# Low weights of two products 32 bytes further on, and their matmul first: a retention and mixture-of-experts kernel

## The chip, the cores and the metric

The kernel runs on one core of a Trainium2 chip. Its time is the device time of one launch in microseconds (us), and a version stands for the median of several runs. PE is TensorE, PEld its weight loads, DVE is VectorE, ACT ScalarE, POOL GpSimd and SP the engine that issues the DMAs.

## The reference, cut to what matters

```python
attn_out = _attn_ref(q, k, v, lam)            # (2, 8, 768, 64): retention with a decaying state
x = attn_out.transpose(0, 2, 1, 3).reshape(1536, 512)
P = balanced(exp(x @ w_gate))                 # 8 rounds of row and column scaling, (1536, 8)
for e in range(8):                            # the part that this change touches
    h = np.maximum(x @ w1[e], 0.0)            # (1536, 512) @ (512, 1024)
    out += P[:, e:e + 1] * (h @ w2[e])        # (1536, 1024) @ (1024, 512)
h = out @ w_in                                # a last dense layer, 512 -> 2048 -> 512
return (h - np.tanh(h)) @ w_out
```

All of it is float32. The kernel keeps float32 accuracy by splitting each operand into a high part (rounded by ScalarE) and a low part (the rest, by VectorE), and adding three matmuls: high by high, high by low, low by high.

## The kernel before, in words

After the attention come 96 steps (`NS`), one for each half of an expert's hidden layer and each of three blocks of 512 tokens. A step computes `x @ w1` by seven products of a Strassen scheme (1, 2, 5, 6, 7, 4, 3, in this order). `product` runs each as six matmuls of 256 columns: for each of the two halves `k` of the inner dimension high by high (L579), high weights by low tokens (L581), low weights by high tokens (L582). The stationary operand is always the weight piece (`w1h`, `w1l`), the moving one the tokens (`xph`, `xpl` for products 1, 2 and 3, `xsh`, `xsl` for the others). Products 1, 6, 7 and 4 are written to `ha`, products 2, 5 and 3 to `hb`.

Twice in a step, ahead of product 7 and ahead of product 4, stand the matmuls of `second` for the step before: 12 of 512 columns each (L477, L478, L480), with the hidden values (`hhia`, `hloa`, `hhib`, `hlob`) stationary, `w2h` and `w2l` moving, and the sums in `yp`. So one step is, on PE: products 1, 2, 5, 6 (24 matmuls), 12 matmuls of `second`, product 7 (6), 12 of `second`, products 4 and 3 (12): 42 short matmuls and 24 long ones, in the order in which the code calls them. Ahead of each matmul stands the load of its weights.

`w1_split` fills the weight tiles some steps ahead: ScalarE copies to `w1h`, VectorE subtracts into `w1l` (L132 and L133 in the helper `split`). `WI` says at which column of the tiles a product's 256 weights begin. In bytes from the start of a partition and modulo 256, the built program has the token tiles at 160, the weight tiles `w1h` and `w1l` at 224, and `w2h`, `w2l` and the hidden tiles at 32. A half of 128 weights is 512 bytes, so all pieces of products 1, 2, 5, 6, 7 and 3 begin at 224, and those of product 4, whose `WI` is 8 columns (32 bytes) more than a multiple of 256, at 0.

```python
WI = {1: 0, 2: 256, 3: 1280, 4: 1536 + 8, 5: 512, 6: 768, 7: 1024}
```

The last dense layer (L686 to L688) has its own weights and is not touched.

Of the kernel before, what the change touches and what calls it, by code (L numbers as in the profile page):

```python
# [8 lines left out]
F32 = mybir.dt.float32  # L9
F32R = mybir.dt.float32r  # L10
# [3 lines left out]
ACTF = mybir.ActivationFunctionType  # L14
ALU = mybir.AluOpType
# [18 lines left out]
PAD = 16  # L34
PADC = 48
W1C = 7 * 256 + 64


TSW = 0.625
# [3 lines left out]

WI = {1: 0, 2: 256, 3: 1280, 4: 1536 + 8, 5: 512, 6: 768, 7: 1024}
XI = {1: ("p", 0), 2: ("p", 1), 3: ("p", 2), 4: ("s", 3), 5: ("s", 0), 6: ("s", 1), 7: ("s", 2)}


# [1 line left out]
def kernel(  # L51
# [9 lines left out]
    nc = tc.nc  # L61
# [5 lines left out]
    wps = [ctx.enter_context(tc.tile_pool(name="wpa", bufs=1))]  # L67
# [28 lines left out]
    wraw, wsum, w1h, w1l, w2h, w2l = {}, {}, {}, {}, {}, {}  # L96
# [8 lines left out]
    def w_sum(q, eng):  # L105
        a11, a12, a22, a21 = (wraw[q][:, 256 * i:256 * i + 256] for i in range(4))
        wsum[q] = stg.tile([128, 1024], F32, tag="sum", name=f"wsum{q}")
        s1, s2, s3, s4 = (wsum[q][:, 256 * i:256 * i + 256] for i in range(4))
        eng.tensor_tensor(out=s1, in0=a21, in1=a22, op=ALU.add)
        eng.tensor_tensor(out=s3, in0=a11, in1=a21, op=ALU.subtract)  # L110
        eng.tensor_tensor(out=s2, in0=s1, in1=a11, op=ALU.subtract)
        eng.tensor_tensor(out=s4, in0=a12, in1=s2, op=ALU.subtract)


    def pad(pool, name, n=PAD):
        if name not in padded:
            padded[name] = pool.tile([128, n], F32, tag=name, name=name)
# [3 lines left out]
    def w1_alloc(q):  # L121
        pad(wps[q % 3], f"pada{q % 3}", (PAD, PAD + 32, PAD + 8)[q % 3])
        w1h[q] = wps[q % 3].tile([128, W1C], F32R, tag="w1h", name=f"w1h{q}")
        w1l[q] = wps[q % 3].tile([128, W1C], F32R, tag="w1l", name=f"w1l{q}")

    def w2_alloc(q):
        pad(wps[q % 3], f"padb{q % 3}")
# [3 lines left out]
    def split(hi, lo, src, eng=nc.vector):  # L131
        nc.scalar.activation(out=hi, in_=src, func=ACTF.Copy)  # L132
        eng.tensor_tensor(out=lo, in0=src, in1=hi.bitcast(F32), op=ALU.subtract)  # L133

    def w1_split(q, part):
        if part == 0:
            w1_alloc(q)
        if q < 2 * NU:
            for o, src in (((WI[1], wraw[q][:, 0:512]), (WI[4], wraw[q][:, 512:768])), ((WI[5], wsum[q]),))[part]:
                n = slice(o, o + src.shape[1])  # L140
                split(w1h[q][:, n], w1l[q][:, n], src)
        else:
            n, m = (slice(c, c + 512) for c in (512 * part, 512 * part + PADC))
            split(w1h[q][:, m], w1l[q][:, m], wraw[q][:, n], nc.gpsimd)
# [36 lines left out]
    for i in range(12):  # L181
# [9 lines left out]
        out=g[:, 129:257], data0=lamt.to_broadcast([H, 128]), data1=one8, initial=1.0,  # L191
# [7 lines left out]
        out=dtab,  # L199
        in_=bass.AP(tensor=gbase.tensor, offset=gbase.offset, ap=[[1, 128], [384, H], [1, 128]]),  # L200
# [3 lines left out]
    for hh in range(2):  # L204
        src = gscr[:, 129:257].rearrange("(n two) m -> two n m", two=2)[hh]
        nc.sync.dma_start(
            out=lq[64 * hh:64 * hh + 64],
            in_=src.rearrange("(o n) m -> o n m", o=1).to_broadcast([64, NP, 128]),
# [9 lines left out]
    scps, at, s1, xr, qd = {}, {}, {}, {}, {}  # L218
# [114 lines left out]
    def gate2(b):  # L333
# [9 lines left out]
    }  # L343
    wt = {
        1: lambda: w_load(0), 3: lambda: w_sum(0, nc.vector), 5: lambda: w1_split(0, 0), 6: lambda: w1_split(0, 1),
        7: lambda: (w2_split(0, 0), w2_split(0, 1), w_load(1)), 10: lambda: w_sum(1, nc.gpsimd),
    }
    def ahead(c):
# [182 lines left out]
    for u in range(NU + NQ):  # L531
        s0 = 6 * (u - 1)
        q0, q1 = 2 * u, 2 * u + 1
        strassen = u < NU
        if u > 0:
            fill[s0 + 2].append(lambda q=q0: w_load(q))
            if strassen:
                fillc[s0 + 2].append(lambda q=q0: w_sum(q, nc.gpsimd))
            s0 += u == 1
            for i in range(2):  # L540
                (fill, fillb)[i][s0 + 3].append(lambda q=q0, i=i: w1_split(q, i))
            for i in range(2):
                (fill, fillb)[i][s0 + 4].append(lambda q=q0, i=i: w2_split(q, i))
            fillb[s0 + 4].append(lambda q=q1: w_load(q))
            if strassen:
                fillc[s0 + 4].append(lambda q=q1: w_sum(q, nc.gpsimd))
            for i in range(2):
                (fill, fillb)[i][s0 + 5].append(lambda q=q1, i=i: w1_split(q, i))
        for i in range(2):
            (fill, fillb)[i][max(s0 + 6, 1)].append(lambda q=q1, i=i: w2_split(q, i))  # L550
# [21 lines left out]
    def product(ps, s, i, start):  # L572
        u, b, p = s // 6, s // 2 % 3, s % 2
        q = 2 * u + p
        kind, xi = XI[i]
        xh, xl = (x1[b][kind, j][:, xi].rearrange("p (k m) -> p k m", k=2) for j in range(2))
        for k in range(2):
            ws = slice(WI[i] + 128 * k, WI[i] + 128 * k + 128)
            nc.tensor.matmul(out=ps, lhsT=w1h[q][:, ws], rhs=xh[:, k], start=start and k == 0, stop=False,  # L579
                             skip_group_check=True)  # L580
            nc.tensor.matmul(out=ps, lhsT=w1h[q][:, ws], rhs=xl[:, k], start=False, stop=False, skip_group_check=True)  # L581
            nc.tensor.matmul(out=ps, lhsT=w1l[q][:, ws], rhs=xh[:, k], start=False, stop=k == 1, skip_group_check=True)  # L582

    pend = None
    for s in range(NS):
# [7 lines left out]
        u, b, p = s // 6, s // 2 % 3, s % 2  # L593
        q = 2 * u + p
        pa, pb = bank(f"ha{s}"), bank(f"hb{s}")
        s12 = sn_.tile([128, 512], F32, tag="s12", name=f"s12_{s}")
        s5 = sn_.tile([128, 256], F32, tag="s5", name=f"s5_{s}")
        lo, hi = slice(0, 256), slice(256, 512)
        product(pa[:, lo], s, 1, True)
        nc.scalar.activation(out=s12[:, lo], in_=pa[:, lo], func=ACTF.Copy)  # L600
        if pend:
            hb = relu_hi(pend[0], f"b{s - 1}")
            lb = relu_lo(pend[0], hb, f"b{s - 1}")
            parts.append(pend[1] + (hb, lb, False, (s - 1) % 2 == 1))
        product(pb[:, lo], s, 2, True)
        product(pb[:, hi], s, 5, True)
        nc.scalar.activation(out=s5, in_=pb[:, hi], func=ACTF.Copy)
        product(pa[:, lo], s, 6, False)
# [35 lines left out]
    def sub(v):  # L644
        u, b, f = NU + v // 12, v // 4 % 3, v % 4
        return u, b, 2 * u + f // 2, f % 2, f
# [32 lines left out]
    for v in range(NV + 2):  # L679
        if v < NV:  # L680
            u, b, q, i, f = sub(v)
            ph = bank(f"g{v}")
            for k in range(KT):
                blk = {(0, 0): 0, (0, 1): 1, (1, 1): 2, (1, 0): 3}[i, k // 2]
                ws = slice(PADC + 256 * blk + 128 * (k % 2), PADC + 256 * blk + 128 * (k % 2) + 128)
# [60 lines left out]
```

## Time and profile before

| what | value |
|---|---|
| median of 3 runs | 1327.33 us (1326.79 to 1328.92) |
| the profiled execution's own time | 1328.56 us |
| its span, first to last instruction | 1326.8 us |
| matmuls on PE | 8383 |
| busy VectorE, ScalarE, GpSimd | 913.0, 527.6 and 274.6 us |
| mean granted TensorE clock | 0.996 |

Matmuls overlap in the records: a record is longer than the distance from its start to the next one's, and its end is modelled. What a matmul costs is read from the starts.

### The profile page before, as it was taken

The numbers are of one execution on the slowest core, as the hardware profiler recorded it, in microseconds if no ns is written. First come the engines' busy times: TensorE is split into PE (matmuls) and PEld (weight loads), VectorE is DVE, ScalarE is ACT, GpSimd is POOL, SyncE is SP. The second block draws the span as 40 slices with busy tenths as digits, with TensorE's granted clock in tenths as the row PEclk, the third lists the DMA queues.
The fourth block names the chain that finished last, engine by engine and source line by source line (L and its number), as shares of the span: only waits on it lengthen the run. The fifth ranks groups of instructions, "written<-read, shape, count | busy, mean of one in ns | idle before, by whom it ended". The sixth has DMA issues, their size and how long they took to land.

```text
span 1326.8 us, 20925 instructions
## 1 busy us (share of the span) xinstructions
PE 1314.7 (99%) x8383; PEld 1163.6 (88%) x8383; DVE 913.0 (69%) x1698; ACT 527.6 (40%) x1029; POOL 274.6 (21%) x323
## 2 busy tenths in 40 slices
PE   8999999999999999999999999999999999999998
PEld 6789999999999999999999999999999888888887
DVE  4976666757667575767666675757654487788887
ACT  1443333223323232323322332323232578776764
POOL 4611011212123131212212221322210102020200
PEclk8999999999999999999999999999999999999999
DMA  9501111212312121212222132221210110010101
GB/s 299 171 33 33 33 61 34 71 56 68 97 46 93 57 68 57 80 56 68 72 64 68 57 99 69 68 68 57 68 36 33 32 33 32 32 32 32 32 33 64
DMA packets 37138, 85.00 MB, mean 64 GB/s; under 512 B 4136, under 2 KB 13872, under 8 KB 37040
## 3 DMA queue, kind: packets, MB, share of 16 engines
q1 hardware_dynamic: 37040, 83.67, 19.8%
q8 instruction: 65, 1.06, 0.3%
q14 instruction: 33, 0.27, 0.1%
HBM read 72.11 MB, written 11.55 MB: 63 GB/s over the span
## 4 chain that ended last, share of the span: by engine, by line
PE 96%; DVE 2%; DMA 1%; issue 0%; ACT 0%; POOL 0%; DVEq 0%; POOLq 0%
PE yp L480 16%; PE yp L477 16%; PE yp L478 16%; PE ha L579 7%; PE ha L582 7%; PE ha L581 7%; PE hb L581 5%; PE hb L579 5%; PE hb L582 5%; PE g L688 3%; PE g L686 3%; PE g L687 3%; PE sc L236 1%; DMA dtab<-gscr 0%; DVE at L242 0%
## 5 line engine op out<-in xcount | busy, mean ns | idle before, releaser
L508 ACT ACTIVATE hhia<-ha 128x512 fp32r<-128x512 f32 x96 | 57.5, 599 | 469.9 <-PE ha L582 464.3
L579 PE MATMUL ha<-xsh,w1h 128*128 128x256 f32 x576 | 162.5, 282 | 1.8 <-ACT s L600 1.3
L582 PE MATMUL ha<-xsh,w1l 128*128 128x256 f32 x576 | 161.3, 280 | 0.0
L581 PE MATMUL ha<-xsl,w1h 128*128 128x256 f32 x576 | 160.9, 279 | 0.0
L456 POOL TENSOR_TENSOR c<-c,d 128x256 f32<-128x256 f32 x64 | 47.8, 747 | 544.3 <-DVE d L455 544.3
L478 PE MATMUL yp<-w2l,hhia 128*128 128x512 f32 x384 | 149.4, 389 | 0.0
L480 PE MATMUL yp<-w2h,hloa 128*128 128x512 f32 x384 | 149.3, 389 | 0.0
L477 PE MATMUL yp<-w2h,hhia 128*128 128x512 f32 x384 | 149.3, 389 | 0.0
L480 PE MATMUL yp<-w2h,hlob 128*128 128x512 f32 x380 | 148.6, 391 | 0.0
L478 PE MATMUL yp<-w2l,hhib 128*128 128x512 f32 x380 | 147.9, 389 | 0.0
L477 PE MATMUL yp<-w2h,hhib 128*128 128x512 f32 x380 | 147.8, 389 | 0.0
L615 DVE TENSOR_TENSOR ha<-ha,s 128x256 f32<-128x256 f32 x96 | 41.4, 432 | 141.8 <-PE ha L582 141.8
L625 DVE TENSOR_TENSOR hb<-hb,s 128x512 f32<-128x512 f32 x96 | 67.0, 698 | 91.3 <-PE hb L582 91.3
L495 DVE SCALAR_TENSOR_TENSOR yacc<-yp,prob,yacc 128x512 f32<-128x512 f32 x168 | 118.8, 747 | 9.0 <-PE yp L480 9.0
L579 PEld LDWEIGHTS ha<-xsh,w1h 128*128 128x128 f32 x576 | 108.4, 188 | 9.6 <-ACT s L600 1.5
L581 PEld LDWEIGHTS ha<-xsl,w1h 128*128 128x128 f32 x576 | 108.5, 188 | 7.4
L582 PEld LDWEIGHTS ha<-xsh,w1l 128*128 128x128 f32 x576 | 109.1, 189 | 0.0
L579 PE MATMUL hb<-xph,w1h 128*128 128x256 f32 x384 | 106.6, 278 | 0.0
L581 PE MATMUL hb<-xpl,w1h 128*128 128x256 f32 x384 | 106.3, 277 | 0.0
L582 PE MATMUL hb<-xph,w1l 128*128 128x256 f32 x384 | 106.1, 276 | 0.0
L480 PEld LDWEIGHTS yp<-w2h,hloa 128*128 128x128 f32 x384 | 72.1, 188 | 15.0
L480 PEld LDWEIGHTS yp<-w2h,hlob 128*128 128x128 f32 x380 | 71.3, 188 | 14.9
(159 smaller groups left out, 3332.6 us busy)
## 6 DMA issues: line engine op xcount, KB each, us to landing
wraw<-in_w SPq DMA_DIRECT2D x64, 512.0 KB, 4.8
d<-in_wio SPq DMA_DIRECT2D x64, 256.0 KB, 2.9
qkv<-in_qkv SPq DMA_DIRECT2D x23, 512.0 KB, 6.9
wscr<-c SPq DMA_DIRECT2D x64, 128.0 KB, 1.8
wraw<-wscr SPq DMA_DIRECT2D x16, 512.0 KB, 4.3
out<-yacc SPq DMA_DIRECT2D x12, 256.0 KB, 2.1
qkv<-in_qkv SPq DMA_DIRECT2D x2, 256.0 KB, 3.3
dtab<-gscr SPq DMA_DIRECT2D x1, 512.0 KB, 6.5
```

The costliest lines, as they stand in the source:

```text
L456: nc.gpsimd.tensor_tensor(out=c1.bitcast(F32), in0=c1.bitcast(F32), in1=lo.bitcast(F32), op=ALU.mult)
L477: nc.tensor.matmul(out=yp, lhsT=a[:, ts], rhs=w2h[q][:, i], start=first, stop=False)
L478: nc.tensor.matmul(out=yp, lhsT=a[:, ts], rhs=w2l[q][:, i], start=False, stop=False)
L480: nc.tensor.matmul(out=yp, lhsT=c[:, ts], rhs=w2h[q][:, i], start=False, stop=last)
L495: nc.vector.scalar_tensor_tensor(out=y, in0=yp[t], scalar=prob[:, b * TPB + t, u // 2:u // 2 + 1], in1=y, op0=ALU.mult, op1=ALU.add)
L508: nc.scalar.activation(out=a, in_=ps, func=ACTF.Relu)
L579: nc.tensor.matmul(out=ps, lhsT=w1h[q][:, ws], rhs=xh[:, k], start=start and k == 0, stop=False, skip_group_check=True)
L581: nc.tensor.matmul(out=ps, lhsT=w1h[q][:, ws], rhs=xl[:, k], start=False, stop=False, skip_group_check=True)
L582: nc.tensor.matmul(out=ps, lhsT=w1l[q][:, ws], rhs=xh[:, k], start=False, stop=k == 1, skip_group_check=True)
L615: nc.vector.tensor_tensor(out=pa[:, hi], in0=pa[:, lo], in1=s5, op=ALU.add)
L625: nc.vector.tensor_tensor(out=pb, in0=pb, in1=s12, op=ALU.add)
L686: nc.tensor.matmul(out=ph, lhsT=w1h[q][:, ws], rhs=x2[b][0][:, k], start=k == 0, stop=False)
```

## The change

It does four things. `LI` gives the low weights a place of their own: for products 7 and 4 the low weights of the first half (`k` = 0) begin at column 1288 and 1608, 32 bytes past the usual place modulo 256, and the second half at the usual one (`w1l` gets 64 columns more). Product 4's high weights, and the second half of its low ones, go back to the usual place. In `product` the matmul with the low weights comes first of the three. To let `w1_split` write the new places, products 3 and 7 trade columns (and `w_sum` two of its slices), and the subtraction for the four summed pieces becomes two instructions.

```diff
--- before.py
+++ after.py
@@ -34,6 +34,7 @@
 PAD = 16
 PADC = 48
 W1C = 7 * 256 + 64
+W1L = 7 * 256 + 128
 
 
 TSW = 0.625
@@ -43,7 +44,11 @@
 
 
 
-WI = {1: 0, 2: 256, 3: 1280, 4: 1536 + 8, 5: 512, 6: 768, 7: 1024}
+
+WI = {1: 0, 2: 256, 3: 1024, 4: 1536, 5: 512, 6: 768, 7: 1280}
+LI = {i: (o, o + 128) for i, o in WI.items()}
+LI[7] = (1288, 1472)
+LI[4] = (1608, 1792)
 XI = {1: ("p", 0), 2: ("p", 1), 3: ("p", 2), 4: ("s", 3), 5: ("s", 0), 6: ("s", 1), 7: ("s", 2)}
 
 
@@ -105,7 +110,7 @@
     def w_sum(q, eng):
         a11, a12, a22, a21 = (wraw[q][:, 256 * i:256 * i + 256] for i in range(4))
         wsum[q] = stg.tile([128, 1024], F32, tag="sum", name=f"wsum{q}")
-        s1, s2, s3, s4 = (wsum[q][:, 256 * i:256 * i + 256] for i in range(4))
+        s1, s2, s4, s3 = (wsum[q][:, 256 * i:256 * i + 256] for i in range(4))
         eng.tensor_tensor(out=s1, in0=a21, in1=a22, op=ALU.add)
         eng.tensor_tensor(out=s3, in0=a11, in1=a21, op=ALU.subtract)
         eng.tensor_tensor(out=s2, in0=s1, in1=a11, op=ALU.subtract)
@@ -121,7 +126,7 @@
     def w1_alloc(q):
         pad(wps[q % 3], f"pada{q % 3}", (PAD, PAD + 32, PAD + 8)[q % 3])
         w1h[q] = wps[q % 3].tile([128, W1C], F32R, tag="w1h", name=f"w1h{q}")
-        w1l[q] = wps[q % 3].tile([128, W1C], F32R, tag="w1l", name=f"w1l{q}")
+        w1l[q] = wps[q % 3].tile([128, W1L], F32R, tag="w1l", name=f"w1l{q}")
 
     def w2_alloc(q):
         pad(wps[q % 3], f"padb{q % 3}")
@@ -136,9 +141,20 @@
         if part == 0:
             w1_alloc(q)
         if q < 2 * NU:
-            for o, src in (((WI[1], wraw[q][:, 0:512]), (WI[4], wraw[q][:, 512:768])), ((WI[5], wsum[q]),))[part]:
-                n = slice(o, o + src.shape[1])
-                split(w1h[q][:, n], w1l[q][:, n], src)
+            def low(i):
+                o, step = LI[i][0], LI[i][1] - LI[i][0]
+                return w1l[q][:, o + 128 - step:o + 128 + step].rearrange("p (k m) -> p k m", k=2)[:, :, step - 128:]
+
+            if part == 0:
+                split(w1h[q][:, 0:512], w1l[q][:, 0:512], wraw[q][:, 0:512])
+                split(w1h[q][:, 1536:1792].rearrange("p (k m) -> p k m", k=2), low(4),
+                      wraw[q][:, 512:768].rearrange("p (k m) -> p k m", k=2))
+            else:
+                nc.scalar.activation(out=w1h[q][:, 512:1536], in_=wsum[q], func=ACTF.Copy)
+                hi = w1h[q].bitcast(F32)
+                nc.vector.tensor_tensor(out=w1l[q][:, 512:1280], in0=wsum[q][:, 0:768], in1=hi[:, 512:1280], op=ALU.subtract)
+                h, w = (a.rearrange("p (k m) -> p k m", k=2) for a in (hi[:, 1280:1536], wsum[q][:, 768:1024]))
+                nc.vector.tensor_tensor(out=low(7), in0=w, in1=h, op=ALU.subtract)
         else:
             n, m = (slice(c, c + 512) for c in (512 * part, 512 * part + PADC))
             split(w1h[q][:, m], w1l[q][:, m], wraw[q][:, n], nc.gpsimd)
@@ -576,10 +592,11 @@
         xh, xl = (x1[b][kind, j][:, xi].rearrange("p (k m) -> p k m", k=2) for j in range(2))
         for k in range(2):
             ws = slice(WI[i] + 128 * k, WI[i] + 128 * k + 128)
-            nc.tensor.matmul(out=ps, lhsT=w1h[q][:, ws], rhs=xh[:, k], start=start and k == 0, stop=False,
+            wl = slice(LI[i][k], LI[i][k] + 128)
+            nc.tensor.matmul(out=ps, lhsT=w1l[q][:, wl], rhs=xh[:, k], start=start and k == 0, stop=False,
                              skip_group_check=True)
-            nc.tensor.matmul(out=ps, lhsT=w1h[q][:, ws], rhs=xl[:, k], start=False, stop=False, skip_group_check=True)
-            nc.tensor.matmul(out=ps, lhsT=w1l[q][:, ws], rhs=xh[:, k], start=False, stop=k == 1, skip_group_check=True)
+            nc.tensor.matmul(out=ps, lhsT=w1h[q][:, ws], rhs=xh[:, k], start=False, stop=False, skip_group_check=True)
+            nc.tensor.matmul(out=ps, lhsT=w1h[q][:, ws], rhs=xl[:, k], start=False, stop=k == 1, skip_group_check=True)
 
     pend = None
     for s in range(NS):
```

On PE, at the end of the first `second` in a step and in product 7 behind it. Before:

```order
L480 MATMUL yp_1_3_6972<-w2h_6664,hloa_7034 128x512
L579 MATMUL ha_7039<-xsh_96,w1h_6335 128x256
L581 MATMUL ha_7039<-xsl_97,w1h_6335 128x256
L582 MATMUL ha_7039<-xsh_96,w1l_6336 128x256
L579 MATMUL ha_7039<-xsh_96,w1h_6335 128x256
L581 MATMUL ha_7039<-xsl_97,w1h_6335 128x256
L582 MATMUL ha_7039<-xsh_96,w1l_6336 128x256
```

And with the change, at the same place:

```order
L496 MATMUL yp_1_3_6992<-w2h_6684,hloa_7055 128x512
L596 MATMUL ha_7060<-xsh_96,w1l_6354 128x256
L598 MATMUL ha_7060<-xsh_96,w1h_6353 128x256
L599 MATMUL ha_7060<-xsl_97,w1h_6353 128x256
L596 MATMUL ha_7060<-xsh_96,w1l_6354 128x256
L598 MATMUL ha_7060<-xsh_96,w1h_6353 128x256
L599 MATMUL ha_7060<-xsl_97,w1h_6353 128x256
```

The matmul with the low weights (`w1l`) moved from third to first in each half, in this and all other products; the number of matmuls is the same. The first L596 is the only one of these six whose weights stand at 0 modulo 256; the others stand at 224. In product 4 it is the same, where before all six stood at 0.

On VectorE, the four-piece subtraction for the same weights (`wsum` are the summed pieces). Before:

```order
L133 TENSOR_TENSOR w1l_1325<-wraw_1109,w1h_1324 128x512
L133 TENSOR_TENSOR w1l_1325<-wraw_1109,w1h_1324 128x256
L133 TENSOR_TENSOR w1l_1325<-wsum_1158,w1h_1324 128x1024
```

And with the change:

```order
L138 TENSOR_TENSOR w1l_1327<-wraw_1111,w1h_1326 128x512
L138 TENSOR_TENSOR w1l_1327<-wraw_1111,w1h_1326 128x2x128
L155 TENSOR_TENSOR w1l_1327<-wsum_1160,w1h_1326 128x768
L157 TENSOR_TENSOR w1l_1327<-wsum_1160,w1h_1326 128x2x128
```

The instruction of 1024 columns became one of 768 and one of 256 in two strips; this happens 32 times. On ScalarE, GpSimd and SP no instruction is added, removed or moved.

## Rows read from the trace of the kernel before

**Rows 1.** The page, part 1 (busy time of engines) and part 4 (chain by engine).

```profile
PE 1314.7 (99%) x8383; PEld 1163.6 (88%) x8383; DVE 913.0 (69%) x1698; ACT 527.6 (40%) x1029; POOL 274.6 (21%) x323
...
PE 96%; DVE 2%; DMA 1%; issue 0%; ACT 0%; POOL 0%; DVEq 0%; POOLq 0%
```

**Rows 2.** Timeline of PE, one step: start, duration, line, matmul.

```profile
559.00 0.39 PE L477 MATMUL yp<-w2h,hhia 128*128 128x512 f32 x1
...
561.72 0.28 PE L579 MATMUL ha<-xsh,w1h 128*128 128x256 f32 x1
...
562.43 0.39 PE L477 MATMUL yp<-w2h,hhib 128*128 128x512 f32 x1
...
564.92 0.40 PE L480 MATMUL yp<-w2h,hlob 128*128 128x512 f32 x1
565.16 0.28 PE L579 MATMUL ha<-xsh,w1h 128*128 128x256 f32 x1
...
565.86 0.28 PE L579 MATMUL hb<-xph,w1h 128*128 128x256 f32 x1
...
566.21 0.28 PE L579 MATMUL hb<-xph,w1h 128*128 128x256 f32 x1
...
569.27 0.39 PE L477 MATMUL yp<-w2h,hhia 128*128 128x512 f32 x1
```

**Rows 3.** Timeline of the weight loads (PEld), same step.

```profile
564.92 0.19 PEld L579 LDWEIGHTS ha<-xsh,w1h 128*128 128x128 f32 x1
565.16 0.19 PEld L581 LDWEIGHTS ha<-xsl,w1h 128*128 128x128 f32 x1
```

**Rows 4.** Groups of PE by form, products 2, 5 and 6: count, busy us, mean ns.

```profile
L582 PE MATMUL hb<-xph,w1l 128*128 128x256 f32 x2 | 0.6, 276 | 0.0
L579 PE MATMUL ha<-xsh,w1h 128*128 128x256 f32 x2 | 0.6, 276 | 0.0
```

**Rows 5.** The same view, the long matmuls ahead of product 7.

```profile
L480 PE MATMUL yp<-w2h,hloa 128*128 128x512 f32 x4 | 1.6, 389 | 0.0
```

**Rows 6.** The same view, product 7.

```profile
L582 PE MATMUL ha<-xsh,w1l 128*128 128x256 f32 x2 | 0.6, 282 | 0.0
L581 PE MATMUL ha<-xsl,w1h 128*128 128x256 f32 x2 | 0.6, 281 | 0.0
L579 PE MATMUL ha<-xsh,w1h 128*128 128x256 f32 x2 | 0.6, 280 | 0.0
L480 PE MATMUL yp<-w2h,hloa 128*128 128x512 f32 x1 | 0.4, 388 | 0.0
```

**Rows 7.** The same view, product 4 (L579: its second) and the long matmul ahead.

```profile
L582 PE MATMUL ha<-xsh,w1l 128*128 128x256 f32 x2 | 0.6, 280 | 0.0
L581 PE MATMUL ha<-xsl,w1h 128*128 128x256 f32 x2 | 0.6, 280 | 0.0
L579 PE MATMUL ha<-xsh,w1h 128*128 128x256 f32 x1 | 0.3, 280 | 0.0
...
L480 PE MATMUL yp<-w2h,hlob 128*128 128x512 f32 x1 | 0.4, 396 | 0.0
```

**Rows 8.** The same view, product 4's last matmul and product 3's first half.

```profile
L582 PE MATMUL ha<-xsh,w1l 128*128 128x256 f32 x1 | 0.3, 283 | 0.0
L579 PE MATMUL hb<-xph,w1h 128*128 128x256 f32 x1 | 0.3, 283 | 0.0
...
L581 PE MATMUL hb<-xpl,w1h 128*128 128x256 f32 x1 | 0.3, 279 | 0.0
L582 PE MATMUL hb<-xph,w1l 128*128 128x256 f32 x1 | 0.3, 277 | 0.0
```

**Rows 9.** Timeline of PE, first matmuls of steps 20 and 90.

```profile
268.62 0.28 PE L579 MATMUL ha<-xph,w1h 128*128 128x256 f32 x1
...
987.76 0.28 PE L579 MATMUL ha<-xph,w1h 128*128 128x256 f32 x1
```

**Rows 10.** Groups by form, VectorE's subtractions into `w1l`, whole program.

```profile
L133 DVE TENSOR_TENSOR w1l<-wsum,w1h 128x1024 fp32r<-128x1024 f32 x32 | 39.7, 1242 | 13.7 <-ACT w1h L132 13.7
...
L133 DVE TENSOR_TENSOR w1l<-wraw,w1h 128x512 fp32r<-128x512 f32 x32 | 24.1, 752 | 6.4 <-ACT w1h L132 6.4
L133 DVE TENSOR_TENSOR w1l<-wraw,w1h 128x256 fp32r<-128x256 f32 x32 | 21.4, 669 | 0.0
```

**Rows 11.** Who waited for whom, PE: total us, times, longest us.

```profile
PE stp L258 <- POOL qkv L227: 4.1, 1, 4.1
PE ha L579 <- ACT s L600: 1.3, 1, 1.3
```

## The prediction

> **What bounds the kernel now.** I read the page first, then the timeline of one step, and last the groups by form in narrow stretches, because the change is a matter of single nanoseconds. The page says that PE is busy for 99% of the span and holds 96% of the chain that ended last [rows 1]. Its waits are few and stand at the start: the longest are 4.1 us on the attention and 1.3 us in the first step [rows 11]. So the time is the sum of the distances from one matmul's start to the next one's, and nothing but a change of these distances, or a new wait on PE, can move it.
>
> The timeline gives the distances. From the second half of product 3 to the end of the next step's product 6 there are 27 matmuls of 256 columns between 566.21 and 569.27, that is 113.3 ns each; 11 long matmuls between 562.43 and 564.92 take 226.4 ns each [rows 2]. But product 7's six take 0.71 us, 118.3 ns each, product 4's six 0.70 us, and the three of product 3's first half 0.35 us, 116.7 ns each [rows 2]. The reader should see that the same instruction in the same shape is 5 ns dearer in one place of the step than in another.
>
> The timeline is printed to 10 ns, so I take single matmuls from the mean length of their records. Where the distance is 113.3, the record is 276 ns [rows 4]; in product 7 the records are 280, 281 and 282 ns [rows 6], on average 5 more, as the distances are. I therefore count a record's excess over 276 (over 389 for a long one [rows 5]) as excess of distance. By this a step now holds:
> - product 7: twice (280 + 281 + 282) less six times 276, 30 ns [rows 6];
> - the long matmul ahead of product 4: 396 against 389, 7 ns [rows 5, 7];
> - product 4: six times 280 less six times 276, 24 ns [rows 7];
> - product 3: 283, 279 and 277, 11 ns, then nothing [rows 8].
>
> That is 72 ns. As a control: 70 steps take 987.76 less 268.62, 10.273 us each [rows 9]; 42 times 113.3 and 24 times 226.4 ns are 10.193 us, so 80 ns are left, which agrees within the rounding of the starts. Over 96 steps 72 ns are 6.9 us, the most that any repair of these places can give.
>
> **What the excess hangs on.** The load of the next weights starts with the running matmul: 564.92 and 565.16 are starts in both views [rows 2, 3]. So at any moment one stream of tokens and one of weights are read together, and what can differ is where they stand. In products 1, 2, 5 and 6 the tokens are at 160 and the weights at 224 modulo 256, and the record is 276. In product 4 the weights are at 0, and it is 280. But product 7 has exactly the addresses of product 6, 160 and 224, and costs 5 ns more per matmul, through all six. So address is not all: there is a state, left behind by the long matmuls (whose operands both stand at 32), that six matmuls at the usual place do not clear. And there is a way out of it, which the trace shows once in each step: behind product 4 the weights return from 0 to 224, the next four records are 283, 283, 279, 277 [rows 8], and from then on the distance is 113.3 up to the next long matmul [rows 2]. The step out costs 7 + 7 + 3 + 1 = 18 ns.
>
> [...]
>
> **The change part by part.** The high weights of product 4 and the second half of its low ones go to the usual place; one weight load of six stays displaced, and it is now the first. Product 7 gets the same. So the load that runs beside the last long matmul is the displaced one, and the first short matmul of the product already runs beside a load at the usual place.
>
> The displaced load's own price is shown only ahead of product 4: 396 against 389, 7 ns [rows 5, 7]. Ahead of product 7, where the record is 388 now [rows 6], the same must come, 8 ns. What follows has no row of its own. The nearest is the return behind product 4, 18 ns over four matmuls, but there six displaced loads went before and here one. The bounds: 0, if the shift is complete with the long matmul, and 18, if the same four steps are needed; no end at all is a rival below. I take 15, near the one return that is shown, a little under it because the records fall fast (7, 7, 3, 1) and part of the shift may be done by the long matmul.
>
> - Product 7 and the long matmul ahead: 8 + 15, and 2 for the last one, beside which the load for the long matmuls starts: 25 instead of 30, a gain of 5 ns.
> - Products 4 and 3 and the long matmul ahead: 7 + 15 = 22 instead of 7 + 24 + 11 = 42, a gain of 20 ns.
>
> Together 25 ns a step, 2.4 us over 96 steps. The first step has no long matmuls and a few others have small ones in between, so I take 2.3.
>
> The low matmul's place as first changes nothing in the other five products: tokens and weights stand at 160 and 224 in each of the three matmuls, whichever comes first. It needs `w1l` earlier, by two matmuls, 0.23 us; the weights are split some steps ahead, and PE's waits name no VectorE instruction there [rows 11]. The trade of products 3 and 7 and the 64 extra columns move addresses by multiples of 256 bytes. VectorE gets 32 more instructions: 1024 columns took 1.24 us and 512 took 0.75 [rows 10], which makes 0.26 us fixed and 0.96 ns per column, so 768 and 256 take 1.00 and 0.51, 0.26 us more each time, 8.4 us in all on an engine that is busy 69% [rows 1]. The cover is that distance in steps; were it gone, each such piece would stall PE by up to 0.26 us.
>
> Sum: 1328.56 (the profiled execution, 1.8 above its span and 1.2 above the median) less 2.3 is 1326.3 for an execution like that one; against the median it is 1327.33 - 2.3 = 1325.0.
>
> **The rivals.**
> 1. *The state does not clear in product 4* (slower). One displaced load is not six: if product 3 still runs in the slow state, nothing else in the program clears it, and it reaches through the next step's products 1, 2, 5 and 6. Products 4 and 3: 7 + 12 x 5 = 67 against 42, 25 more; 24 matmuls x 5 = 120 more; product 7: 8 + 30 against 30, 8 more. 153 ns a step, 14.7 us: 1342.0. For it: product 7 shows that the state holds for six matmuls at the usual place. Against it: the displaced load shifts the long matmul by 7 ns already today. It is decided in product 3: 281 or 276.
> 2. *The state clears at once.* The tail is the first 7 or nothing: with 7, product 7 costs 8 + 7 + 2 = 17 and product 4 with 3 costs 14, a gain of 13 + 28 = 41 ns, 3.9 us, 1323.4; with nothing, 7 less in each place, the gain is 55 ns, 5.3 us, 1322.0.
> 3. *It clears in product 4 but not in 7.* Gain 20, loss 8: 12 ns, 1.2 us, 1326.2. For it: the two places follow different long matmuls, and only one has ever been seen to clear.
> 4. *Nothing happens*: what I read as address and state is the order of the work, and the time stays 1327.3. Against it stands product 4 as the one place with other addresses and other records [rows 7]. [...]
>
> **How the numbers follow.** The forecast (a tail of 12 to 18 ns, 1324.3 to 1325.5) gets 0.46, rival 1 0.13, rival 2 0.21, rival 3 0.12, rival 4 0.06, and 0.02 is left for a late `w1l`. A measurement of this kernel can tell about 0.2%, 2.65 us, from no change, so faster begins below 1324.7. There lie rival 2 and somewhat over a third of the forecast: 0.38. Slower are rival 1 and the late weights, with a little for rounding: 0.16. The rest, 0.46, is the same. The range goes from 1322.5, which leaves out the far end of rival 2, to 1327.6, which takes in rivals 3 and 4 and leaves out rival 1.
>
> **What the profile of the changed kernel would show.** The long matmul ahead of product 7 should have a record near 396 instead of 388. In products 7 and 4 the records should fall towards 276 from the first half to the second, and all of product 3 should be at 276. The matmuls on `hb` should all have a mean of 276. If product 3 and the next step's products 1 to 6 stand near 281, rival 1 is true; if product 7's second half is at 281 and product 4's at 276, rival 3. I would be wrong if the way out needs more than one displaced load, or if it is the long run at 0 and not the return from it that clears the state.

## The result, and the profile after

The changed kernel takes 1339.22 us (median of 4 runs, 1337.78 to 1341.32), against 1327.37 for the kernel before (1326.79 to 1328.92). The ratio is 1.009, with a 95% interval from 1.0077 to 1.0102. So it is 11.85 us slower, where 1325.0 with a range up to 1327.6 was forecast. The profiled execution took 1339.07 us, with a span of 1337.3. Of the versions below, `p4_two` was profiled in an execution with a mean granted clock of 0.654 (span 1876.2 us) in place of 1.00, so only its times are read.

The page of the changed kernel, its parts 1, 4 and 5 (the last: line, engine, matmul, count, busy us, mean ns, idle us):

```profile
PE 1323.5 (99%) x8383; PEld 1172.5 (88%) x8383; DVE 916.2 (69%) x1730; ACT 527.8 (39%) x1029; POOL 273.8 (20%) x323
...
PE 95%; DVE 2%; DMA 1%; issue 1%; SPq 0%; ACT 0%; DVEq 0%
...
L596 PE MATMUL hb<-xph,w1l 128*128 128x256 f32 x384 | 108.0, 281 | 0.0
```

The bound is where it was [rows 1]: PE is busy for 99% of the span with the same 8383 matmuls. But PE's busy time grew by 8.8 us, and the matmuls on `hb` (products 2 and 3 in the row shown; product 5's have the same mean) have a mean record of 281 ns. This is the row in which the prediction said that it would be decided: 276 if product 4 leads out of the state in which product 7 runs, 281 if not.

The timeline of PE in the changed kernel, one step and the starts of the next step and of step 90 (start, duration, line, matmul), answers to [rows 2, 9]:

```profile
581.49 0.28 PE L596 MATMUL ha<-xph,w1l 128*128 128x256 f32 x1
...
584.32 0.39 PE L493 MATMUL yp<-w2h,hhia 128*128 128x512 f32 x1
...
586.81 0.40 PE L496 MATMUL yp<-w2h,hloa 128*128 128x512 f32 x1
587.05 0.28 PE L596 MATMUL ha<-xsh,w1l 128*128 128x256 f32 x1
...
587.75 0.39 PE L493 MATMUL yp<-w2h,hhib 128*128 128x512 f32 x1
...
590.48 0.28 PE L596 MATMUL ha<-xsh,w1l 128*128 128x256 f32 x1
...
591.18 0.28 PE L596 MATMUL hb<-xph,w1l 128*128 128x256 f32 x1
...
591.89 0.28 PE L596 MATMUL ha<-xph,w1l 128*128 128x256 f32 x1
...
997.49 0.28 PE L596 MATMUL ha<-xph,w1l 128*128 128x256 f32 x1
```

Between 581.49 and 584.32 stand the 24 matmuls of products 1, 2, 5 and 6. They are 117.9 ns apart, where 27 such distances took 113.3 each before [rows 2]: some 110 ns more per step. The 11 long ones from 584.32 to 586.81 take 226.4 ns each, as before. Product 3 takes 0.71 us, 0.02 more than before. The step from 581.49 to 591.89 is 10.40 us long, and 40 steps (997.49 less 581.49) give 10.400 each, against 10.273 [rows 9]. That is 127 ns more; over 95 steps it makes 12.1 us, about the measured loss. So nearly all of the loss lies in the spacing of short matmuls, most of it in four products whose addresses the change leaves alone; the long matmul ahead of product 7 adds some 9 ns a step (its record is 397 below, 388 in [rows 6]).

Groups of PE by form in the changed kernel (count, busy us, mean ns, idle us): product 7 with the long matmul ahead; product 4's first half, then its second half; the first matmul of product 3. They answer to [rows 6 to 8]:

```profile
L598 PE MATMUL ha<-xsh,w1h 128*128 128x256 f32 x2 | 0.6, 282 | 0.0
L599 PE MATMUL ha<-xsl,w1h 128*128 128x256 f32 x2 | 0.6, 281 | 0.0
L596 PE MATMUL ha<-xsh,w1l 128*128 128x256 f32 x2 | 0.6, 279 | 0.0
L496 PE MATMUL yp<-w2h,hloa 128*128 128x512 f32 x1 | 0.4, 397 | 0.0
...
L598 PE MATMUL ha<-xsh,w1h 128*128 128x256 f32 x1 | 0.3, 281 | 0.0
L599 PE MATMUL ha<-xsl,w1h 128*128 128x256 f32 x1 | 0.3, 281 | 0.0
L596 PE MATMUL ha<-xsh,w1l 128*128 128x256 f32 x1 | 0.3, 277 | 0.0
...
L598 PE MATMUL ha<-xsh,w1h 128*128 128x256 f32 x1 | 0.3, 282 | 0.0
...
L596 PE MATMUL ha<-xsh,w1l 128*128 128x256 f32 x1 | 0.3, 281 | 0.0
...
L596 PE MATMUL hb<-xph,w1l 128*128 128x256 f32 x1 | 0.3, 281 | 0.0
```

Read it in the order of the program, where L596 is the first of each three. Ahead of product 7 the long matmul rises to 397, as forecast (396). In product 4 the first short matmul has 277, and for one matmul it looks as if the state were gone. But the next has 281, and so it goes on, through product 3, into the next step. Behind six displaced loads the records fell (283, 283, 279, 277 in [rows 8]); behind one they fall once and return.

VectorE's pieces came a little cheaper than estimated (0.97 and 0.45 us by the groups of the changed kernel, in place of 1.00 and 0.51). These are PE's longest wait and the longest one of a step (total us, times, longest us):

```profile
PE stp L274 <- POOL qkv L243: 3.8, 2, 3.2
...
PE ha L596 <- ACT s L617: 0.7, 1, 0.7
```

No wait of a step names VectorE, so the split's cost stays covered.

### The profile page after: what moved, and what is told of

Same layout as the page of the kernel before. It is cut to its first block, busy times and chain, and to the rows that moved or that the text cites. A ratio compares the mean times of both kernels' runs of the same rounds, so it can differ in the third digit from the quotient of the medians.

```text
span 1337.3 us, 20956 instructions
## 1 busy us (share of the span) xinstructions
PE 1323.5 (99%) x8383; PEld 1172.5 (88%) x8383; DVE 916.2 (69%) x1730; ACT 527.8 (39%) x1029; POOL 273.8 (20%) x323
## 4 chain that ended last, share of the span: by engine, by line
PE 95%; DVE 2%; DMA 1%; issue 1%; SPq 0%; ACT 0%; DVEq 0%
PE yp L496 16%; PE yp L493 16%; PE yp L494 16%; PE ha L596 7%; PE ha L599 7%; PE ha L598 7%; PE hb L596 5%; PE hb L598 5%; PE hb L599 5%; PE g L705 3%; PE g L703 3%; PE g L704 3%; DMA qkv<-in_qkv 1%; DVE at L258 1%; PE tr L539 0%
## 5 line engine op out<-in xcount | busy, mean ns | idle before, releaser
L596 PE MATMUL ha<-xsh,w1l 128*128 128x256 f32 x576 | 163.0, 283 | 1.2 <-ACT s L617 0.7
L596 PEld LDWEIGHTS ha<-xsh,w1l 128*128 128x128 f32 x576 | 108.2, 188 | 8.9 <-ACT s L617 0.9
L596 PE MATMUL hb<-xph,w1l 128*128 128x256 f32 x384 | 108.0, 281 | 0.0
```

Source lines behind the costliest of these rows:

```text
L596: nc.tensor.matmul(out=ps, lhsT=w1l[q][:, wl], rhs=xh[:, k], start=start and k == 0, stop=False, skip_group_check=True)
```

## The experiments

**What was to be told apart.** The theory: within a step, the state that the long matmuls leave behind is left only by displaced loads, one is not enough, and all that the change costs comes from product 4. The rivals: the new order (low matmul first), product 7's part, and that some other number of displaced loads, or another distance, leads out as the prediction assumed. In all kernels of the first two groups the program is the one before except for the lines shown and for `w1_split`, which writes the weights to the columns named. "Step" in the table is the difference of the starts of steps 50 and 90, divided by 40, as read from the timeline of each.

| kernel | displaced loads in product 4 | step, us | product 3's record, ns | median, us | ratio to before, 95% |
|---|---|---|---|---|---|
| before | 6 | 10.273 | [rows 8] | 1327.37 | |
| after (product 7 also one) | 1 | 10.400 | 281 | 1339.22 | 1.0077 to 1.0102 |
| `order_only` | 6 | 10.273 | as before | 1326.71 | 0.9987 to 1.0005 |
| `p4_none` | 0 | 10.387 | 281 | 1337.83 | 1.0060 to 1.0094 |
| `p4_one` | 1 | 10.393 | 281 | 1337.50 | 1.0060 to 1.0088 |
| `p4_two` | 2 | | | 1342.05 | 1.0097 to 1.0130 |
| `p4_three` | 3 | 10.247 | 276 | 1324.50 | 0.9966 to 0.9986 |
| `p4_four` | 4 | 10.427 | 281 | 1341.46 | 1.0092 to 1.0123 |
| `p4_five` | 5 | 10.393 | 282, 281 | 1338.50 | 1.0067 to 1.0107 |
| `p4_one64` | 1, by 64 bytes | 10.427 | 281 | 1341.84 | 1.0095 to 1.0130 |
| `both_three` | 3, and 3 in product 7 | 10.240 | 276 | 1325.17 | 0.9977 to 0.9996 |

### The order alone, and product 4 alone

`order_only` is the kernel before with the low matmul first of the three in every product:

```diff
-            nc.tensor.matmul(out=ps, lhsT=w1h[q][:, ws], rhs=xh[:, k], start=start and k == 0, stop=False,
+            nc.tensor.matmul(out=ps, lhsT=w1l[q][:, ws], rhs=xh[:, k], start=start and k == 0, stop=False,
...
-            nc.tensor.matmul(out=ps, lhsT=w1h[q][:, ws], rhs=xl[:, k], start=False, stop=False, skip_group_check=True)
-            nc.tensor.matmul(out=ps, lhsT=w1l[q][:, ws], rhs=xh[:, k], start=False, stop=k == 1, skip_group_check=True)
+            nc.tensor.matmul(out=ps, lhsT=w1h[q][:, ws], rhs=xh[:, k], start=False, stop=False, skip_group_check=True)
+            nc.tensor.matmul(out=ps, lhsT=w1h[q][:, ws], rhs=xl[:, k], start=False, stop=k == 1, skip_group_check=True)
```

> The kernel before with one edit: in every product the matmul with the low weights comes first; all addresses are as before. Theory 1 (what decides is how the loads at the displaced place follow each other): no change, 1327.3 us, product 3's second half and products 1, 2, 5 and 6 at records of 276 ns. Rival (the order of the three matmuls keeps the slow state alive): about 1339 us, with records near 281 ns in products 1 to 6.

It took 1326.71 us beside 1326.89 for the kernel before, and its step is the same to the nanosecond. The order costs nothing and gives nothing.

`p4_one` has product 4 as in the change (one displaced load, the first) and product 7 as before. `HI4` and `LO4` are the columns of the two halves of product 4's weights; 1544 and 1672 lie 32 bytes past the usual place, 1536, 1664 and 1728 at the usual one. The kernels named `p4_` differ in these tuples (`p4_none` has none); `p4_one`, `p4_four` and `p4_one64` also run product 4's low matmul first, so that the displaced loads stand together at its head.

```diff
-WI = {1: 0, 2: 256, 3: 1280, 4: 1536 + 8, 5: 512, 6: 768, 7: 1024}
+WI = {1: 0, 2: 256, 3: 1280, 4: 1536, 5: 512, 6: 768, 7: 1024}
+HI4, LO4 = (1536, 1664), (1544, 1728)
...
+            if i == 4:
+                ws, wl = slice(HI4[k], HI4[k] + 128), slice(LO4[k], LO4[k] + 128)
```

> The kernel before with product 4 as in the change (one displaced load, the first; low weights first in product 4 alone); product 7 as before. Theory 1 (the slow state is left or not behind product 4): 1338.6 us, the changed kernel's 1339.2 less some 0.6 us for product 7, all of products 3, 1, 2, 5 and 6 near 281 ns. Rival (the displaced load ahead of product 7 is the harm): about 1325.5 us, product 3 falling to 276 ns.

It took 1337.50 us, 10.6 of the change's 11.85 us. Its records on `hb` in the page:

```profile
L594 PE MATMUL hb<-xph,w1h 128*128 128x256 f32 x384 | 107.9, 281 | 0.0
```

The place of product 4's weights alone carries the loss into the other products (the row is that of products 2 and 3). What is left, 127 less 120 ns per step by the two step lengths, 0.7 us, is product 7's part: its long matmul goes from 388 to 397 and nothing clears.

### How many displaced loads lead out

In the same way, from the kernel before:

```diff
+HI4, LO4 = (1544, 1728), (1536, 1664)
+HI4, LO4 = (1544, 1728), (1544, 1728)
+HI4, LO4 = (1544, 1728), (1544, 1672)
+HI4, LO4 = (1544, 1672), (1544, 1728)
+HI4, LO4 = (1536, 1664), (1552, 1728)
+WI = {1: 0, 2: 256, 3: 1280, 4: 1536, 5: 512, 6: 768, 7: 1024}
```

These are, in this order, `p4_two` (the first half's high weights, which two matmuls load), `p4_three` (the whole first half), `p4_four` (low first; the first half and the second's low), `p4_five` (the first half and the second's high), `p4_one64` (one load, low first, by 64 bytes) and, with this line alone, `p4_none`.

> The kernel before with product 4's first-half high weights displaced and everything else in it at the usual place: two displaced loads. After three, the matmul behind the second displaced one ran at once at 113.3 ns. Theory 1a (the place in the sequence decides): two leads back one matmul earlier, from a distance of 118.3 and not of 116.7, so as with one or four it stays slow, 1337 to 1341 us. Theory 1b' (any number but one, if the first half holds them all, clears): 1324 to 1325 us.

> The kernel before with the first half of product 4's weights displaced, high and low, and the second half at the usual place: three displaced loads, order as before. Theory 1a (the state goes round in a cycle of three loads, since product 4's records before repeat after three, and only its third place leads out): it clears as after six, product 4 with 3 costs some 10 ns a step less than before, 1326.4 us. Theory 1b (clearing needs many displaced loads): it stays slow, about 1339 us.

> The kernel before with four displaced loads in product 4: low weights first in product 4, first half all displaced, of the second half the low weights alone. Theory 1a (cycle of three loads): four is like one, it stays slow, about 1339 us. Theory 1b (enough displaced loads clear it; three or four are enough if three are): 1326.5 to 1327 us.

Two did not lead out (by its time, which is just above the range expected), three did, and four did not. `p4_three` is 2 us faster than expected. Its rows by form: product 4's first half, its second half, the first matmul of product 3.

```profile
L592 PE MATMUL ha<-xsh,w1h 128*128 128x256 f32 x1 | 0.3, 279 | 0.0
L592 PE MATMUL ha<-xsl,w1h 128*128 128x256 f32 x1 | 0.3, 279 | 0.0
L592 PE MATMUL ha<-xsh,w1l 128*128 128x256 f32 x1 | 0.3, 276 | 0.0
...
L592 PE MATMUL ha<-xsh,w1h 128*128 128x256 f32 x1 | 0.3, 276 | 0.0
...
L592 PE MATMUL hb<-xph,w1h 128*128 128x256 f32 x1 | 0.3, 276 | 0.0
```

The records are 279, 279, and from the third matmul on, beside which the return to the usual place is loaded, 276. There is no tail at all: with three loads the return costs nothing. Whether the third displaced load or the return behind it clears the state can't be told, as the first clean record is the one beside the return. In `p4_four`, where the low matmul comes first (by form, product 4's first and second half), the third record is no longer clean, and the state is back at once:

```profile
L594 PE MATMUL ha<-xsh,w1l 128*128 128x256 f32 x1 | 0.3, 279 | 0.0
L594 PE MATMUL ha<-xsh,w1h 128*128 128x256 f32 x1 | 0.3, 279 | 0.0
L594 PE MATMUL ha<-xsl,w1h 128*128 128x256 f32 x1 | 0.3, 278 | 0.0
...
L594 PE MATMUL ha<-xsh,w1h 128*128 128x256 f32 x1 | 0.3, 281 | 0.0
L594 PE MATMUL ha<-xsl,w1h 128*128 128x256 f32 x1 | 0.3, 281 | 0.0
L594 PE MATMUL ha<-xsh,w1l 128*128 128x256 f32 x1 | 0.3, 278 | 0.0
```

After this the theory was that the loads go round in threes: only behind the third of a round does the return fall on a clean moment, which the six of the kernel before, two rounds, meet too. Five and none were the numbers to try it on, and one load by another distance. A round that starts without the state comes under "One distance for all loads".

> Five displaced loads at the head of product 4: the first half's and the second half's high weights; only the second half's last is at the usual place. Theory that the state goes round in three matmuls and is left only after the third of a round (three and six displaced loads clear, one, two and four don't): five stays in it, like two, 1337 to 1342 us, products 3, 1, 2, 5 and 6 at 117 ns and more. Rival, that it takes a number of them, or that four is the exception: five clears, 1325 to 1327 us.

> As the run with one displaced load in product 4 and product 7 as before, but that load's weights lie 64 bytes further on modulo 256 (at 32) in place of 32. Theory that only the number of displaced loads counts: stays in the state, 1337 to 1338 us. Rival, that the displacement sets in which of the round's places a matmul ends: one load by 64 bytes may lead out, 1324 to 1326 us.

> No displaced load in the program: product 4's weights all at the usual place, the order and the rest as in the kernel before. It completes the series of 0, 1, 2, 3, 4, 5 and 6 displaced loads (1, 2, 4 and 5 stayed in the state, 3 and 6 left it). Theory that displaced loads, three at a time, are the only way out: all of the short matmuls behind the long ones stand 117 to 118 ns from one another, products 3, 1, 2, 5 and 6 too, 1336 to 1342 us. Rival, that nothing needs clearing and the shorter run would do without any displaced load (the long matmuls or product 3 leave the state by themselves): product 4 as product 7, 30 ns, product 3 and the next four clean, 1322 to 1325 us.

Five stayed in the state, as the round of three says and "enough of them" does not; by form, the first matmul of product 3 in `p4_five`:

```profile
L592 PE MATMUL hb<-xph,w1h 128*128 128x256 f32 x1 | 0.3, 282 | 0.0
```

One load by 64 bytes stayed in too, and cost 4.3 us more than one by 32, above the range expected; of that, some 3 us are in the steps (10.427 against 10.393), where the 12 long matmuls ahead of product 7 take 2.75 us instead of 2.72. None at all costs as much as one (1337.83 and 1337.50): the displaced load of the change bought nothing in product 4. Without any, the state set by the long matmuls holds through all 42 short ones of a step (product 3's records are 281, and the 24 behind it, in step 2 below, are 117.9 ns apart), so product 4 of the kernel before is a repair, worth 10.5 us, and the change took it away.

The start of `p4_none` shows the state being set. Timeline of PE: products 2 and 5 of step 0 begin, product 3 of step 0, step 1 and its first matmul of `second`, and the same two of step 2.

```profile
61.59 0.28 PE L579 MATMUL hb<-xph,w1h 128*128 128x256 f32 x1
...
62.30 0.28 PE L579 MATMUL hb<-xsh,w1h 128*128 128x256 f32 x1
...
68.61 0.28 PE L579 MATMUL hb<-xph,w1h 128*128 128x256 f32 x1
...
69.29 0.28 PE L579 MATMUL ha<-xph,w1h 128*128 128x256 f32 x1
...
72.01 0.39 PE L477 MATMUL yp<-w2h,hhia 128*128 128x512 f32 x1
...
79.79 0.28 PE L579 MATMUL ha<-xph,w1h 128*128 128x256 f32 x1
...
82.62 0.39 PE L477 MATMUL yp<-w2h,hhia 128*128 128x512 f32 x1
```

In step 1, before the program's first matmul of `second`, the 24 matmuls of products 1, 2, 5 and 6 take 2.72 us, 113.3 ns each; in step 2, behind 24 long ones, the same take 2.83. So the addresses of the short ones alone don't make them slow. But the long ones are not the only thing that sets the state: product 2 of step 0, behind the small matmuls of the attention, takes 0.71 us for six (61.59 to 62.30), where the same six take 0.68 in the kernel before (61.31 to 61.99 in its timeline). Nor are displaced loads the only way out: product 3 of step 0 takes 0.68 us, and between the two stand, besides products 5, 6, 7 and 4, two waits of PE (1.3 and 0.5 us) and 32 small matmuls, but no displaced load. Which of these leads out, and what sets the state ahead of product 2, no run here tells apart.

### Three in both products

`both_three` displaces the first half's high and low weights in products 7 and 4 alike (each half's columns from `WK`):

```diff
+WI = {1: 0, 2: 256, 3: 1024, 4: 1608, 5: 512, 6: 768, 7: 1288}
+WK = {i: (o, o + (184 if i in (7, 4) else 128)) for i, o in WI.items()}
...
-            ws = slice(WI[i] + 128 * k, WI[i] + 128 * k + 128)
+            ws = slice(WK[i][k], WK[i][k] + 128)
```

> Three displaced loads (the first half, high and low) at the head of product 4 and of product 7. Theory 1a: product 7 clears as product 4 did; its excess falls from 28 to 21 ns a step with the long matmul ahead of it (8 + 5 + 3, then 113.3 ns, and 4 at the last), so 0.5 us less than with product 4 alone: 2.9 us under before, about 1324. Rival (product 7 follows other long matmuls and doesn't clear): product 7 at 118 ns and the displaced load paid on top, 1325.2.

Product 7 with the long matmul ahead, by form in `both_three`:

```profile
L588 PE MATMUL ha<-xsh,w1h 128*128 128x256 f32 x2 | 0.6, 278 | 0.0
L590 PE MATMUL ha<-xsl,w1h 128*128 128x256 f32 x2 | 0.6, 278 | 0.0
L591 PE MATMUL ha<-xsh,w1l 128*128 128x256 f32 x2 | 0.6, 277 | 0.0
L489 PE MATMUL yp<-w2h,hloa 128*128 128x512 f32 x1 | 0.4, 396 | 0.0
```

Three loads clear product 7 as well: 278, 278, 277 where one load left 282, 281, 279. But the long matmul pays 8 ns for it, so the step is only 7 ns shorter than that of `p4_three`, 0.6 us in all, less than the times can tell: 1325.17 beside 1327.68, 1324.50 beside 1326.89. The time alone would fit the rival, 1325.2; the records decide. These two are the versions that beat both kernels, `p4_three` by 0.14 to 0.34% against the kernel before, `both_three` by 0.04 to 0.23%.

### One distance for all loads

If displaced loads only repair what the change of places between long and short matmuls breaks, one distance for all should need no repair. `one_distance` has everything that moves at 160 and everything stationary at 224, `w2` and the hidden tiles and the last layer too; `one_dist_reset` adds `p4_three`'s displaced half to it; `zero_distance` has all at 160. The core of the edit (pads and columns; the first line for `one_distance`, the second for `zero_distance`):

```diff
-        pad(wps[q % 3], f"pada{q % 3}", (PAD, PAD + 32, PAD + 8)[q % 3])
+        pad(wps[q % 3], f"pada{q % 3}", (PAD, PAD + 48, PAD + 40)[q % 3])
...
+        pad(wps[q % 3], f"pada{q % 3}", (PAD + 48, PAD + 48, PAD + 24)[q % 3])
```

> The tiles of the long matmuls moved too: all moving operands at 160 and all stationary ones at 224 modulo 256, in the steps and in the last layer, product 4 at the usual place. Theory 2 (the slow state is set when the pair of places changes, at the switch between short and long matmuls): no switch, no excess: 73 ns a step less, 7 us, and some 1 us in the last layer: 1319 us. Rival (anything that stops PE can set it too, and nothing here clears it): the small matmuls of steps 1 to 11 leave it slow for the rest, 1335 us or more.

> The same with product 4's first half displaced by 32 bytes, high and low, as a way out in each step. Theory 2 with stops that set the state: each step clears it at product 4 at a price of 15 to 25 ns, 1321 to 1322 us, and better than one_distance if that one stays slow. Rival (three displaced loads set the state when it isn't there): slower than before, up to 1340 us.

> All moving and all stationary tiles lie at the same place modulo 256, 160, the hidden tiles, the second matrix's weights and the last layer too; no load is displaced from another. Theory that no load at one and the same place collides, as the long matmuls of the kernel before show for themselves (w2 and the hidden tiles both at 32): every short matmul stands 113.3 ns behind the one ahead of it and every long one 226.5, the 73 ns per step that the kernel before has over these spacings go, 96 x 73 ns = 7.0 us, so 1319 to 1321 us. Rival: the short ones collide at this place in every load, by the 4 to 5 ns of the state: 42 x 4.2 ns = 175 ns per step in place of 73, 96 x 102 ns = 10 us more, 1335 to 1345 us.

They took 1341.69 (ratio 1.0101 to 1.0129), 1343.16 (1.0110 to 1.0139) and 1348.57 us (1.0147 to 1.0182), all slower, where 1319 to 1322 were expected, and for reasons of interest. Timeline of PE, `one_distance`, the first matmul of a step, and the first and the seventh of the long ones behind product 6:

```profile
578.90 0.28 PE L580 MATMUL ha<-xph,w1h 128*128 128x256 f32 x1
...
581.62 0.39 PE L478 MATMUL yp<-w2h,hhia 128*128 128x512 f32 x1
...
583.02 0.39 PE L478 MATMUL yp<-w2h,hhia 128*128 128x512 f32 x1
```

The 24 short ones from 578.90 to 581.62 are 113.3 ns apart, and the mean record on `hb` in its page is 276 ns over all 384 of each line: with no displaced load anywhere, the state of the short ones is gone together with the change of distance, and with it the need of a repair. But the long ones, at the distance of 64 bytes that suits the short ones, are 233 ns apart (581.62 to 583.02, six of them) instead of 226.4, which loses more than was won; the last layer's long matmuls, over a thousand, lose 6.1 us with them (264.7 us instead of 258.6 from its first matmul's start to that of its last on `g`). With that, `one_dist_reset`'s displaced loads have nothing to clear and cost 13 ns a step (10.373 less 10.360).

They show something else. Product 4 of `one_dist_reset` by form, its third matmul and its second half:

```profile
L593 PE MATMUL ha<-xsh,w1l 128*128 128x256 f32 x1 | 0.3, 283 | 0.0
...
L593 PE MATMUL ha<-xsh,w1h 128*128 128x256 f32 x1 | 0.3, 283 | 0.0
L593 PE MATMUL ha<-xsl,w1h 128*128 128x256 f32 x1 | 0.3, 279 | 0.0
L593 PE MATMUL ha<-xsh,w1l 128*128 128x256 f32 x1 | 0.3, 277 | 0.0
```

Three displaced loads, begun without the state, end without it (product 3's records are 276), after a tail of 283, 283, 279 and 277 ns. That is the tail of the kernel before to the nanosecond [rows 8]. So its six loads read as two rounds: the first three clear the state, as in `p4_three`, and the second three start clean and leave this tail, which clears nothing. `p4_four` and `p4_five`, with one and two loads beyond a round, then set the state anew. This reading fits every row; no run starts one or two loads without the state by themselves.

Timeline of PE, `zero_distance`, the first matmul of a step and the first, seventh and twelfth long one:

```profile
585.71 0.28 PE L579 MATMUL ha<-xph,w1h 128*128 128x256 f32 x1
...
588.59 0.40 PE L477 MATMUL yp<-w2h,hhia 128*128 128x512 f32 x1
...
589.98 0.39 PE L477 MATMUL yp<-w2h,hhia 128*128 128x512 f32 x1
...
591.11 0.39 PE L480 MATMUL yp<-w2h,hloa 128*128 128x512 f32 x1
```

Here the short ones are all slow, 2.88 us for 24, 120 ns each, the slowest of all; of the long ones the first six are 232 ns apart and the next five 226. The rival of this run was true in kind, but the price was above its range: 6.7 ns for each short matmul instead of 4 to 5, and the long ones pay too. Of these two distances each kind wants another, and the kernel before has that: 64 bytes for the short ones, none for the long.

## Why the prediction was wrong

- **What bounds the kernel**: right. PE carries the time, and only the distances of its matmuls changed; neither VectorE's pieces nor the earlier need of `w1l` made a wait, and the order is neutral (`order_only`).
- **That there is a state beside the address, set by the long matmuls**: right, though in `p4_none` it also stands behind other work (118 ns in product 2 of step 0). `p4_none` shows it set by the first long ones (113.3 ns for each short one in step 1, 117.9 in step 2) and then through the whole step, and `one_distance` shows that it goes when long and short ones have one distance of 64 bytes (113.3 ns again). The place counts for itself too: the same 24 short matmuls are 113.3 ns apart in `one_distance` and 120 in `zero_distance`.
- **The displaced load's own price**, 8 ns on the long matmul ahead of product 7: right, 397 against 388, 9 ns.
- **The step that failed**: "The nearest is the return behind product 4, 18 ns over four matmuls, but there six displaced loads went before and here one … I take 15". I took the difference of six and one for a matter of size, between 0 and 18 ns, and left "no end at all" to rival 1 with 0.13. It is a matter of which number: none, one, two, four and five displaced loads don't lead out, three and six do. And the tail of 18 ns was misread as the way out: `one_dist_reset` has the same tail where there is no state to leave, and in `p4_three` the state is gone by the third matmul with no tail. With one load, in place of a tail of 15 ns the state stays on every short matmul up to the next long ones, and the step is 127 ns longer. The prediction's own condition, that it would be wrong "if the way out needs more than one displaced load", is what happened.
- **Rival 1** was the outcome, 1342.0 worked out and 1339.22 measured, with the place named rightly (product 3 at 281). Its 153 ns a step were 127. Its term that was mis-sized is the excess by records: the 24 matmuls ahead of the long ones were put at 5 ns each, 120, and measured 4.6 by their starts, some 110. The rest, 33 ns by records, is 17 by step length. "I therefore count a record's excess over 276 … as excess of distance" overstates it; starts over a long run of matmuls, which I had, are the better measure.
- **Rival 2 and 3** need a state that clears in product 4; with one load it doesn't. With three loads rival 2's "clears at once" is nearly what `p4_three` and `both_three` show, 26 and 33 ns a step shorter than before, where rival 2 had 41 to 55 with one load.

What stays open: why the round is three loads long. That is a regularity over seven numbers (0 to 6) behind 12 long matmuls with operands at 32, and of three without the state, with one displacement; no run here shows what in the chip it stands for. Whether another displacement has another round is open too: 64 bytes were tried with a single load only.

## What to carry to other kernels

Where matmuls of one shape have two spacings in a trace, look for what came before them as well as for their addresses: one stretch can set a state that many later ones pay for (here 24 matmuls, 117.9 ns each in place of 113.3), and a place that looks dear can be the repair of it. Before thinning such a repair, count: a trace that shows the repair with six loads says nothing of one, and the price of losing it was here not the repair's own 20 to 40 ns but the state's 4.6 ns times every matmul behind it. Take costs of single nanoseconds from starts over many matmuls, not from record lengths: here 33 ns by records were 17 by step length.

## What the runs showed of the hardware that was not expected

- The number of displaced loads, from 0 to 6, acts in threes: 3 and 6 give steps of 10.247 and 10.273 us, 0, 1, 4 and 5 give 10.387 to 10.427, and 2 gives 1342.05 us as a whole, like 4.
- The distance between moving and stationary data modulo 256 bytes acts on the two shapes in opposite ways, as far as 64 bytes and none go, at the places of these two runs: at 64 bytes (`one_distance`) 113.3 ns for 256 columns, where no state is set, and 233 for 512; at none (`zero_distance`) 120 and, after six at 232, 226.
- The long matmuls can slow down too: in `p4_four` the 12 ahead of product 7 take 2.75 us (584.83 to 587.58 in its timeline) in place of 2.72 [rows 2], and the step is 40 ns longer than without any displaced load (10.427 against 10.387). `p4_one64` does the same, `p4_one` and `p4_five` don't; what tells them apart is open.
- The state stands behind other work than the long matmuls, and is left by other work than displaced loads, at the start of `p4_none` (118 ns in product 2 of step 0, then 113.3 in its product 3, with no displaced load).
